# High parts of eight weight blocks taken from ScalarE to GpSimd, and the kernel's order planned anew

## The chip, the core and the metric

The kernel runs on one core of one Trainium2 chip. The metric is the device time of one execution in microseconds; the median of the three runs before the change is 571.56 us (571.51 to 574.22).

## What is computed

A block-sparse attention is followed by a channel mixer. The attention has 4 batches, 8 heads, 768 positions of 64 features, in blocks of 32 positions (24 blocks). Block rows 0 and 23 see all positions; each other row of blocks sees its two neighbours, itself, blocks 0 and 23, and three sampled blocks.

```python
scores = scale * np.matmul(q, k.transpose(0, 1, 3, 2))
mask = np.abs(blk_i - blk_j) <= window
mask = mask | (blk_i == 0) | (blk_j == 0) | (blk_i == n_blocks - 1) | (blk_j == n_blocks - 1)
# and the three sampled blocks of each row of blocks
attn = softmax(np.where(mask, scores, -1e9))
x = (attn @ v) as (batch, position, 512)
xk = mu_k * x + (1.0 - mu_k) * x_prev        # x_prev: the position before
xr = mu_r * x + (1.0 - mu_r) * x_prev
k = np.maximum(xk @ w_k, 0.0)                # w_k 512 x 1024
v = k * k @ w_v                              # w_v 1024 x 512
r = 1.0 / (1.0 + np.exp(-(xr @ w_r)))        # w_r 512 x 512
return r * v
```

The mixer's weights arrive as 64-bit floats; the kernel makes 32-bit numbers of them itself.

## The kernel before

**Attention.** There are 26 units of work (L267). Units 0 to 3 are the "wide" ones, one for each batch: block rows 0 and 23 against all positions. Units 4 to 25 are the "near" ones: one row of blocks for all four batches. A unit loads its queries (L462, DMA) and GpSimd scales them (L464); it needs keys (KA) and values (VA), which lie in two fixed tensors. The wide units fill half of KA and VA each, the near units use the same room as a ring of block slots, so a load has to wait until the matmuls that read the old contents are done. A wide unit does scores (L607), row maxima on VectorE (L616), exponentials on ScalarE (L622), transposes on TensorE (L526) with a copy out by ScalarE or VectorE (L530, L532), and the product with the values (L637). A near unit does the same in L562, L570, L542, L526, L530 and L586. finish (L646) divides by the sum (L655 to L659) and transposes into the mixer's input tiles xt (L666 to L688).

**Weights.** w_r, w_k and w_v are 20 blocks of 128 x 512: blocks 0 to 3 are w_r, 4 to 11 w_k, 12 to 19 w_v. Each block (weight, L359) is loaded as 64-bit words (L365): blocks 0 to 11 into a buffer of their own (early_w), the last eight into slots of the pool "p", which the exponentials use as well (raw). ScalarE makes a magnitude of the upper word (L374), VectorE makes the 32-bit number in three passes: a shift (L379), the sign (L383) and the tail (L387), into wf. Then the number is split in two parts for the matmuls: the high part is a rounding copy, on GpSimd (L397) for the blocks that HI_POOL (L888) names, which are 0 to 11, and on ScalarE (L399) for blocks 12 to 19; the low part is wf less the high part, on GpSimd (L401).

**Mixer.** There are 12 tiles of 256 positions. For each, split_x (L714) makes xr and xk with a difference on GpSimd (L738), a multiply-add on VectorE (L741), a rounding copy on ScalarE (L748) and a remainder on GpSimd (L750). gate does the matmuls of r (L774), hidden those of k (L792) with ReLU and square on ScalarE (L805, L806) and square and remainder on GpSimd (L807, L809), values those with w_v (L821), whose result VectorE multiplies by the gate (L829) before it is stored (L832). TensorE's work of tile t begins with the matmuls r{t}_0; they are called r0_0, r1_0 and so on here.

**Order.** Nothing is issued where it stands in the code. Each operation is added to a Plan (L86) with an engine, an assumed duration in ns, a due time (rank), the buffers that it reads and writes, and, for a load, a size. Plan.order (L190) plays the operations through with these durations and picks, for each engine, the one with the earliest due time among those that can start about then; the result is the fixed program order of each engine. The due times come from a table of numbers at the end of the file (L899 to L909): the start of each unit and tile, offsets for each kind of step, and the due times of the weights' loads (RAW_AT) and passes (WEIGHT_AT). Each engine runs its list in order and waits on semaphores, so an operation that has to wait holds up all that is behind it on its engine. SyncE (SP) issues all loads in one such list.

## Time and profile before

| | |
|---|---|
| median of the three runs | 571.56 us |
| the profiled execution's own time | 573.36 us |
| its span, first to last instruction | 571.5 us |
| busy in the span: TensorE | 538.0 us (94%) |
| busy: VectorE, ScalarE, GpSimd | 262.3, 295.2, 317.1 us |
| read from HBM | 78.60 MB |

The profiled execution took 573.36 us, 1.8 us more than the median run; its span leaves out 1.86 us around the instructions. Where a view has columns for the engines, PE is TensorE, PEld its weight loads, DVE VectorE, ACT ScalarE, POOL GpSimd, and SPq the queue of SyncE that issues DMAs. In the timeline a row has its start, its length (both us), the engine, the line, the operation, output <- input, and in brackets the idle time just before it with what ended that. In the groups by line the last columns are total busy us, mean ns of one, and the idle time before. L numbers are lines of the kernel before; in the changed kernel the same statements stand 17 lines further down (L401 is L418 there).

### The profile page before, as it was taken

To read this page: it belongs to the slowest core of one execution; us is meant where nothing else is said; L and a number is where in the kernel's file an instruction comes from. 1 tells how busy PE (TensorE), PEld (TensorE's weight loads), DVE (VectorE), ACT (ScalarE), POOL (GpSimd) and SP (SyncE) were. 2 spreads that over 40 slices of the span, in tenths; PEclk is the share of its full clock that TensorE was granted. 3 is DMA by queue.
4 is the path that set the end of the run, shared out by engine and by line. 5 is a ranking of instruction groups with operands and counts; after the bars stand their busy time and mean duration, and the time that the engine had idled before them with its cause. 6 is when DMAs were issued, how large, how long until landed. Compare 5 with 4: busy or idle time off the path is not lost.

```text
span 571.5 us, 18262 instructions
## 1 busy us (share of the span) xinstructions
PE 538.0 (94%) x7724; PEld 441.8 (77%) x7724; DVE 262.3 (46%) x481; ACT 295.2 (52%) x594; POOL 317.1 (55%) x377
## 2 busy tenths in 40 slices
PE   8678768999999999999999999999999999999997
PEld 3445545777797897897897887897798898989896
DVE  1677998864434324337325345415434424242401
ACT  2536477675656445467456456556555543424241
POOL 1322657897465384475275456466167265677670
PEclk8979998999999999999999999999999999999999
DMA  8999899734442624454543272445323000000001
GB/s 319 367 387 367 303 315 346 267 120 147 133 148 78 220 77 129 154 169 132 194 142 114 93 225 89 146 160 188 117 89 95 21 21 19 18 21 18 33 5 38
DMA packets 34181, 86.08 MB, mean 151 GB/s; under 512 B 5010, under 2 KB 5780, under 8 KB 31124
## 3 DMA queue, kind: packets, MB, share of 16 engines
q1 hardware_dynamic: 34100, 84.92, 44.2%
q8 instruction: 61, 1.00, 0.7%
q14 instruction: 20, 0.16, 0.1%
HBM read 78.60 MB, written 6.29 MB: 149 GB/s over the span
## 4 chain that ended last, share of the span: by engine, by line
PE 75%; DMA 9%; POOL 7%; DVE 4%; SPq 3%; issue 2%; ACT 1%; POOLq 0%; ACTq 0%
PE v L821 23%; PE o L586 7%; PE s L562 6%; PE t L526 6%; PE r_0p L774 5%; PE h_0p L792 5%; PE r_1p L774 5%; PE h_3p L792 5%; PE h_2p L792 5%; PE h_1p L792 5%; DMA q<-qt 3%; DMA VA<-vw 2%; DMA KA<-kt 2%; POOL q L464 2%; PE tx L666 2%
## 5 line engine op out<-in xcount | busy, mean ns | idle before, releaser
L821 PE MATMUL v<-wv,k 128*128 128x512 f32 (+1 forms) x600 | 144.8, 391 | 1.1 <-POOL wv L401 1.1
L821 PEld LDWEIGHTS v<-wv,k 128*128 128x128 f32 x600 | 106.6, 188 | 24.5 <-POOL wv L401 1.5
L542 ACT ACTIVATE p<-s,nm 128x256 f32<-128x256 f32 x176 | 71.7, 484 | 20.6 <-DVE nm L570 20.5
L464 POOL TENSOR_SCALAR q<-q 128x512 f32<-128x512 f32 (+1 forms) x26 | 36.6, 1409 | 45.8 <-DMA q<-qt 25.1
L570 DVE TENSOR_REDUCE nm<-s 128x4 f32<-128x1024 f32 x44 | 52.8, 1217 | 13.5 <-PE s L562 13.1
L530 ACT COPY pt<-t 128x512 f32<-128x512 f32 x68 | 39.6, 587 | 37.4 <-PE t L526 34.8
L526 PE MATMUL t<-ident,p 128*128 128x128 f32 x352 | 54.5, 278 | 3.8 <-ACT pt L530 2.1
L586 PEld LDWEIGHTS o<-VA,pt 128*32 128x32 f32 x2816 | 42.2, 109 | 13.3 <-issue 10.4
L586 PE MATMUL o<-VA,pt 128*32 128x65 f32 x2816 | 49.5, 222 | 2.9 <-ACT pt L530 1.9
L526 PEld LDWEIGHTS t<-ident,p 128*128 128x128 f32 x352 | 40.6, 141 | 14.8 <-ACT pt L530 2.9
L562 PE MATMUL s<-KA,q 64*32 64x256 f32 x1408 | 44.9, 383 | 4.0 <-DMA KA<-kt 1.7
L750 POOL TENSOR_TENSOR xr<-xr_1f,xr 128x256 fp32r<-128x256 f32 x24 | 17.9, 744 | 38.5 <-ACT xr L748 38.5
L829 DVE SCALAR_TENSOR_TENSOR z<-v,z 128x512 f32<-128x512 f32 (+1 forms) x25 | 16.7, 669 | 48.4 <-PE v L821 48.4
L741 DVE SCALAR_TENSOR_TENSOR xr_1f<-xr_1d,mk,xt 128x128 f32<-128x128 f32 x48 | 17.1, 355 | 47.5 <-POOL xr L750 39.7
L738 POOL TENSOR_TENSOR xr_1d<-xt 128x128 f32<-128x128 f32 x48 | 20.5, 427 | 31.8 <-DVE xr_1f L741 24.0
L792 PE MATMUL h_1p<-xk,wk 128*128 128x256 f32 x288 | 36.9, 282 | 0.0
L562 PEld LDWEIGHTS s<-KA,q 64*32 64x32 f32 x1408 | 25.2, 106 | 15.1 <-issue 2.4
L792 PE MATMUL h_0p<-xk,wk 128*128 128x256 f32 x288 | 36.8, 282 | 0.0
L774 PE MATMUL r_0p<-wr,xr 128*128 128x512 f32 x144 | 36.7, 400 | 0.0
L792 PE MATMUL h_3p<-xk,wk 128*128 128x256 f32 x288 | 36.5, 281 | 0.0
L792 PE MATMUL h_2p<-xk,wk 128*128 128x256 f32 x288 | 36.1, 281 | 0.0
L738 POOL TENSOR_TENSOR xr_0d<-xt 128x128 f32<-128x128 f32 x48 | 19.4, 403 | 30.1 <-DVE xr_0f L741 20.7
(138 smaller groups left out, 962.4 us busy)
## 6 DMA issues: line engine op xcount, KB each, us to landing
VA<-vt SPq DMA_DIRECT2D x93, 260.0 KB, 3.8
KA<-kt SPq DMA_DIRECT2D x90, 256.0 KB, 3.7
VA<-vw SPq DMA_DIRECT2D x24, 260.0 KB, 6.5
KA<-kq SPq DMA_DIRECT2D x16, 384.0 KB, 6.4
out<-z SPq DMA_DIRECT2D x23, 256.0 KB, 2.0
q<-qt SPq DMA_DIRECT2D x22, 256.0 KB, 4.3
early_w<-w_k SPq DMA_DIRECT2D x8, 512.0 KB, 7.3
raw<-w_v SPq DMA_DIRECT2D x8, 512.0 KB, 6.1
```

Of the source, the lines that this page charges most:

```text
L464: plan.add(POOL, 90 + 0.95 * HP * many * BLK, due, lambda: nc.gpsimd.tensor_scalar(out=q.ap[:, 0 : HP * many * BLK], in0=q.ap[:, 0 : HP * ...
L526: nc.tensor.transpose(tp.ap[:, i, :], p.ap[:, x : x + P], ident.ap)
L530: plan.add(ACT, 200 + 0.75 * P * many, rank + 0.1, lambda: nc.scalar.copy(pt.ap[:, 0:many], tp.ap[:, 0:many]), reads=[(tp,)], writes=[(pt,)])
L542: plan.add(ACT, 262 + 0.83 * width, rank, lambda: nc.scalar.activation(p.ap[:, out], view(), AF.Exp, bias=nm()), reads=[(s,), key[0]], wri ...
L562: nc.tensor.matmul(s.ap[ROWS[j], row, a * 256 : (a + 1) * 256].rearrange("p (c x t) -> p c t x", c=2, t=QB), q.ap[half, (hp * QB + j) * BL ...
L570: nc.vector.tensor_reduce(out=nm.ap.rearrange("p (r a) -> p r a", r=2), in_=s.ap.rearrange("p r (a x) -> p r a x", a=2), axis=AX.X, op=ALU ...
L586: nc.tensor.matmul(o[gi].ap[ROWS[j], i * DV : (i + 1) * DV], pts[row].ap[:, 2 * a + g, ROWS[j]], VA.ap[:, c0 + g, j, h * DV : (h + 1) * DV ...
L738: sub.tensor_tensor(out=parts(d.ap), in0=cols(c, 0), in1=cols(c, 1), op=ALU.subtract)
L750: plan.add(POOL, 80 + 2.4 * MIX * tw, rank + O_MIX, lambda f=f, cs=cs: nc.gpsimd.tensor_tensor(out=dst.ap[:, 1, cs], in0=f.ap, in1=dst.ap[ ...
L774: nc.tensor.matmul(pr.ap[:, 0:512], xr.ap[:, a, c, :], wr.ap[:, w, c, :], start=(c == 0 and m == 0), stop=(c == CC - 1 and m == 2))
L792: nc.tensor.matmul(ph.ap[:, ff * TT : (ff + 1) * TT], wk.ap[:, w, c, f * P : (f + 1) * P], xk.ap[:, a, c, :], start=(c == 0 and m == 0), s ...
L821: nc.tensor.matmul(pv.ap[:, 0:width], k2.ap[:, a, f, i * P : (i + 1) * P], wv.ap[:, w, f, cs], start=(f == 0 and m == 0), stop=(f == FC - ...
```

## The change

It has three parts. First, HI_POOL names blocks 0 to 19: the rounding copy of the eight blocks of w_v goes from ScalarE to GpSimd. Second, the planner's durations are changed: VectorE's passes over the weights, its multiply-adds and the packing of the sampled indices get a factor "slow", by which they are lengthened for the time in which an operation of over 300 ns stands on GpSimd beside them; some base durations and sizes of loads are changed, and the scaling of the queries is taken as 2.45 ns a column, where it was 0.95. Third, all numbers of the due-time table are new. No operation is added or removed, and apart from the eight copies none changes its engine; what each engine runs, and in which order, comes from the new plan.

```diff
+    def beside(self, at, ns, slow):
+
+        end = at + ns
+        for _ in range(4):
+            end = at + ns + slow * sum(max(0.0, min(end, b) - max(at, a)) for a, b in self.pool[-6:])
+        return end
...
+            if op.engine == "DVE":
+                vector = op
+                if op.slow:
+                    op.end = self.beside(at, ns, op.slow)
+            if op.engine == "POOL" and op.ns > 300:
+                self.pool.append((at, op.end))
+                if vector is not None and vector.slow and vector.end > at:
+                    vector.end += vector.slow * (min(vector.end, op.end) - at)
+                    free["DVE"] = vector.end
...
-                     writes=[(raw,)], release=at, size=524288)
+                     writes=[(raw,)], release=at, size=455000)
...
-            plan.add(DVE, 480, rank, shift, reads=[(mag,)], writes=[(mag,)])
-            plan.add(DVE, 800, rank, sign, reads=[(mag,), (raw,)], writes=[(mag,)])
-            plan.add(DVE, 800, rank, tail, reads=[(mag,), (raw,)], writes=[(f,)])
+            plan.add(DVE, 430, rank, shift, reads=[(mag,)], writes=[(mag,)], slow=0.53)
+            plan.add(DVE, 690, rank, sign, reads=[(mag,), (raw,)], writes=[(mag,)], slow=0.35)
+            plan.add(DVE, 690, rank, tail, reads=[(mag,), (raw,)], writes=[(f,)], slow=0.35)
...
-            plan.add(POOL, 700, rank, lambda: nc.gpsimd.tensor_copy(dst()[:, 0, :], f.ap), reads=[(f,)], writes=[(owner, (0, key))])
+            plan.add(POOL, 650, rank, lambda: nc.gpsimd.tensor_copy(dst()[:, 0, :], f.ap), reads=[(f,)], writes=[(owner, (0, key))])
...
-        plan.add(POOL, 90 + 0.95 * HP * many * BLK, due, lambda: nc.gpsimd.tensor_scalar(
+        plan.add(POOL, 90 + 2.45 * HP * many * BLK, due, lambda: nc.gpsimd.tensor_scalar(
...
-                plan.add(DVE, 2.8 * tw, rank + O_MIX, mix, reads=[(d,), (x, *ready), (mk, which)], writes=[(f, i)])
+                plan.add(DVE, 220 + 1.02 * tw, rank + O_MIX, mix, reads=[(d,), (x, *ready), (mk, which)], writes=[(f, i)], slow=0.55)
...
-HI_POOL = frozenset(range(12))
+HI_POOL = frozenset(range(20))
...
-LEAD_W, LEAD_Q, LEAD_K, LEAD_V = 9.086, 41.427, 90.995, -12.936
+LEAD_W, LEAD_Q, LEAD_K, LEAD_V = 33.654, 70.566, 88.255, -1.014
...
```

What the new plan does at three places, as the programs have it. In each piece a row is one instruction or a run of equal ones (x2), with its line, its operation, the output tile <- its inputs, and the shape.

SyncE's list before, where the keys of units 4 and 5 are loaded (KA<-kt are keys, VA<-vw values of a wide unit, raw14 is block 14, which is of w_v, q5 the queries of unit 5; the rows of L491 fetch a sampled block; the last row is the last part of unit 5's keys):

```order
L491 REGISTER_ALU x2
L491 ISA
L491 DMA KA_67<-kt 128x512
L365 DMA raw14_918<-w_v 128x1024
L462 DMA q5_945<-qt 128x512
L444 DMA KA_67<-kt 128x512
```

The same place now:

```order
L508 DMA KA_67<-kt 128x512
L479 DMA q5_848<-qt 128x512
L491 DMA VA_68<-vw 128x520 x2
L382 DMA raw16_912<-w_v 128x1024
L382 DMA raw14_919<-w_v 128x1024
L491 DMA VA_68<-vw 128x520 x4
L382 DMA raw19_962<-w_v 128x1024
L461 DMA KA_67<-kt 128x512
```

The six loads of unit 2's values, which stood ahead of unit 4's keys, now stand behind them, and three blocks of w_v instead of one stand ahead of the end of unit 5's keys.

GpSimd's list before, from the scaling of unit 8's queries on (xr0 and xk0 belong to the mixer's tile 0, xr1 to tile 1):

```order
L464 TENSOR_SCALAR q8_1481<-q8_1481 128x512
L401 TENSOR_TENSOR wv_1305<-wf12_1572,wv_1305 128x512
L738 TENSOR_TENSOR xr0_1d0_1679<-xt0_99 128x128
L750 TENSOR_TENSOR xk0_1544<-xk0f1_1585,xk0_1544 128x512
L738 TENSOR_TENSOR xr0_1d1_1736<-xt0_99 128x128
L738 TENSOR_TENSOR xr0_1d2_1758<-xt0_99 128x128
L750 TENSOR_TENSOR xr0_1_1761<-xr0_1f0_1700,xr0_1_1761 128x256
L401 TENSOR_TENSOR wv_1305<-wf18_1743,wv_1305 128x512
```

The same place now, from a few rows ahead of it:

```order
L414 CAST wv_1104<-wf15_1517 128x512
L767 TENSOR_TENSOR xk0_1554<-xk0f0_1488,xk0_1554 128x512
L418 TENSOR_TENSOR wv_1104<-wf15_1517,wv_1104 128x512
L755 TENSOR_TENSOR xk0d3_1630<-xt0_100 128x256
L481 TENSOR_SCALAR q8_1503<-q8_1503 128x512
L755 TENSOR_TENSOR xr0_1d0_1662<-xt0_100 128x128
L767 TENSOR_TENSOR xk0_1554<-xk0f1_1605,xk0_1554 128x512
L755 TENSOR_TENSOR xr0_1d1_1756<-xt0_100 128x128
L755 TENSOR_TENSOR xr0_1d2_1767<-xt0_100 128x128
L767 TENSOR_TENSOR xr0_1_1769<-xr0_1f0_1718,xr0_1_1769 128x256
L414 CAST wv_1104<-wf12_1765 128x512
L418 TENSOR_TENSOR wv_1104<-wf12_1765,wv_1104 128x512
```

Before, blocks 14 and 13 of w_v are done ahead of the row of q8, and blocks 12, 18, 16, 15, 17 and 19 follow it; now blocks 16, 14, 19, 13 and 15 are ahead of it, each with its copy, and blocks 12, 17 and 18 follow.

ScalarE's list before, around the copy of unit 7's first transposed piece (pt7_0_0), which lies behind three copies of w_v:

```order
L399 CAST wv_1305<-wf18_1743 128x512
L542 ACTIVATE p7_0_1767<-s7_0_1546,nm7_0_1608 128x256 x4
L805 ACTIVATE h0_0k_1807<-h0_0p_1745 128x512
L399 CAST wv_1305<-wf16_1790 128x512
L748 CAST xr0_1_1761<-xr0_1f1_1785 128x256
L806 ACTIVATE k20_1825<-h0_0k_1807 128x512
L530 COPY pt7_0_0_1841<-t7_0_0_1816 128x512
L399 CAST wv_1305<-wf15_1839 128x512
L530 COPY pt7_0_1_1874<-t7_0_1_1849 128x512
```

The same place now:

```order
L391 ACTIVATE wmag18_1830<-raw18_1716 128x512
L822 ACTIVATE h0_0k_1835<-h0_0p_1771 128x512
L823 ACTIVATE k20_1850<-h0_0k_1835 128x512
L765 CAST xr0_1_1769<-xr0_1f1_1805 128x256
L822 ACTIVATE h0_1k_1872<-h0_1p_1815 128x512
L559 ACTIVATE p7_1_1876<-s7_1_1607,nm7_1_1855 128x256 x4
L547 COPY pt7_0_0_1901<-t7_0_0_1879 128x512
L823 ACTIVATE k20_1850<-h0_1k_1872 128x512
L547 COPY pt7_0_1_1983<-t7_0_1_1949 128x512
```

The copies of w_v are gone from ScalarE; the exponentials of unit 7's second half (p7_1) have come ahead of pt7_0_0.

TensorE's list has the same matmuls ahead of r1_0 in both programs, in another order, and so the same ones behind it: ahead of it are all of the four wide units, 12 half units of scores (L562), 9 half units of values (L586), two gates (L774), the whole hidden part (L792) and the values part (L821) of tile 0. Ahead of r0_0 stand the same matmuls too, but for one group of four transposes (tx5, L666), which has gone behind it.

More of the change, by code (lines that the diff above doesn't have):

```diff
@@ L82 @@
 class Op:
-    __slots__ = ("engine", "ns", "lag", "fn", "rank", "deps", "users", "bufs", "end", "start", "table", "seq", "waits", "release", "size", "code", "dmas")
+    __slots__ = ("engine", "ns", "lag", "fn", "rank", "deps", "users", "bufs", "end", "start", "table", "seq", "waits", "release", "size", "code", "dmas", "slow")
 class Plan:
@@ L98, in __init__, with add @@
         self.queues = {}
-    def add(self, engine, ns, rank, fn, reads=(), writes=(), lag=0, table=None, release=0.0, size=0, code=0, dmas=1):
+    def add(self, engine, ns, rank, fn, reads=(), writes=(), lag=0, table=None, release=0.0, size=0, code=0, dmas=1, slow=0.0):
         op = Op()
@@ L105, in add @@
         op.deps, op.users, op.end, op.seq = set(), [], None, len(self.ops)
[L106 removed]
+        op.bufs, op.release, op.size, op.code, op.dmas, op.slow = [], release * 1000, size, code, dmas, slow
         for used, *keys in list(reads) + list(writes):
@@ L188, in run @@
         return self.work(end, ns * left / op.code)
+    def beside(self, at, ns, slow):
[3 more added lines that the diff above has]
+        return end
     def order(self):
+        self.pool, vector = [], None
         free, table, avail = {}, {}, {}
@@ L337, in pack @@
             v.tensor_tensor(out=packed.ap, in0=packed.ap, in1=whole[:, 0], op=ALU.bitwise_or)
-        plan.add(DVE, 5500, PICK, pack, reads=[(number,), (con,)], writes=[(r,), (e,), (packed,)])
+        plan.add(DVE, 5500, PICK, pack, slow=0.3, reads=[(number,), (con,)], writes=[(r,), (e,), (packed,)])
         for w, m in enumerate((mu_k, mu_r)):
@@ L474, in load_unit @@
                 plan.add(SP, ISSUE, at - LEAD_V, lambda g=g, c=c, part=part: nc.sync.dma_start(VA.ap[:, c, part], vw[b, g]),
-                         writes=[(VA, *[(c, part, j) for j in range(QB)])], release=at - LEAD_V, size=262144)
+                         writes=[(VA, *[(c, part, j) for j in range(QB)])], release=at - LEAD_V, size=232000)
             return q, None
@@ L897 @@
 LAST = 10
[L899 to L909 removed]
+O_MAX, O_EXP, O_TR = [729.96, 1068.75, -2659.26, 720.02], [22.35, 294.96, -481.10, 448.11], [1.48, 12.00, -243.38, -329.90]
+O_PV, O_END = [-1189.67, -125.48, -1258.70, -1272.22], [32.92, 33.70, 13.31, 331.96]
+SECOND = [7.03, 5.67, -4.63, -100.88]
+LEAD_W, LEAD_Q, LEAD_K, LEAD_V = 33.654, 70.566, 88.255, -1.014
+O_MIX, O_SQ, O_SQ_FIRST = -281.947, 1284.146, 357.911
+NEAR, STAY, STORE = 53.833, 180.777, 639.005
+UNIT_AT = [9.41, -675.38, 18.42, -388.80, 24.44, 48.97, 67.31, 88.69, 97.05, 113.73, 134.30, 147.42, 156.50, 171.87, 187.87, 208.43, 220.91, 234.15, 244.48, 264.65, 275.88, 284.12, 297.62, 339.83, 349.70, 358.79]
+MIX_AT = [79.62, 120.69, 156.49, 190.62, 227.79, 259.66, 283.93, 326.47, 362.70, 747.53, 1179.69, 1656.28]
+MIX_RATE, MIX_RATE_LAST = 1.336, 7.459
+RAW_AT = [-168.17, -329.88, -731.29, 48.63, -279.08, -219.72, -171.89, 46.34, -171.78, -945.78, -1540.07, -21.87]
+WEIGHT_AT = [4.98, -256.20, -1869.62, -233.34, -353.74, -136.35, -216.79, -196.53, -243.10, -202.23, -808.80, -274.05, 82.19, 27.81, -30.53, 59.38, -106.03, 96.35, 105.21, 27.22]
 def kernel(**inputs):
```

13 lines of the change are left out of this document (1 added, 12 removed).

## Prediction

> **What bounds the kernel now.** First the page: how busy TensorE is over the 40 slices of the span, at which clock, and how busy the DMA engines are.
>
> ```profile
> span 571.5 us, 18262 instructions
> ...
> PE   8678768999999999999999999999999999999997
> ...
> PEclk8979998999999999999999999999999999999999
> DMA  8999899734442624454543272445323000000001
> ```
>
> TensorE is full from the eighth slice on, to the last. The DMA engines are full in the first seven slices and not after them. So there are two regimes, and the change can work only where TensorE has holes. Next the stretches, cut at the start of r0_0 and of r1_0 (53 us is a cut for the loads, below), and the timeline rows that give the cuts.
>
> ```profile
> core 0: us, PE busy (x) PEld busy (x) DVE busy (x) ACT busy (x) POOL busy (x), PEclk, DMA share, GB/s
> 0.00:53.00 53.00, 39.84 (x665) 22.35 (x666) 29.10 (x58) 21.77 (x35) 13.79 (x21) 0.90 0.97 361
> 53.00:101.20 48.20, 36.17 (x924) 24.32 (x924) 45.09 (x69) 32.45 (x70) 29.08 (x31) 0.96 0.90 319
> 101.20:147.70 46.50, 43.02 (x656) 35.11 (x655) 30.46 (x52) 28.27 (x56) 37.71 (x38) 1.00 0.50 167
> 147.70:571.50 423.80, 418.98 (x5485) 359.99 (x5483) 157.69 (x304) 212.76 (x434) 236.56 (x288) 1.00 0.33 103
> ```
>
> ```profile
> 101.23 1.65 PE L774 MATMUL r_0p<-wr,xr 128*128 128x512 f32 x6
> ...
> 147.50 2.81 PE L774 MATMUL r_0p<-wr,xr 128*128 128x512 f32 x11
> ```
>
> Three stretches follow from this.
>
> The first ends at r0_0, at 101.2 us. TensorE has 25.2 us of holes (101.2 less 39.84 and 36.17), the DMA engines are 97% and 90% busy, and from 53 us on VectorE is busy for 45.09 of 48.20 us. Keys, values and weights must come in before the mixer can run.
>
> The second goes from r0_0 to r1_0 and takes 46.5 us. TensorE has 3.5 us of holes, and GpSimd is the next fullest engine with 37.71 us.
>
> The third, to the end, has 4.8 us without TensorE, of which 3.3 us lie behind its last matmul (the last gate product and store, untouched).
>
> The waits of TensorE in the second stretch and in the third name the holes:
>
> ```profile
> PE t L526 <- ACT pt L530: 1.8, 1, 1.8
> PE v L821 <- POOL wv L401: 1.1, 1, 1.1
> PE t L526 <- ACT h_3k L805: 0.4, 1, 0.4
> PE t L526 <- ACT h_0k L805: 0.2, 1, 0.2
> ...
> PE t L526 <- ACT z L781: 1.0, 1, 1.0
> PE o L586 <- DVE xk5f L741: 0.4, 1, 0.4
> ```
>
> Both orders have the same matmuls ahead of r1_0, and so the same ones behind it. Hence the end moves by as much as r1_0 moves, plus what the waits of the third stretch gain or lose. The sum is made that way.
>
> **The eight copies.** The prices of one block's steps, from the groups by line (total us, mean ns of one):
>
> ```profile
> L379 DVE TENSOR_SCALAR wmag<-wmag 128x512 int32<-128x512 int32 x20 | 14.7, 750 | 3.3 <-ACT wmag L374 3.3
> L401 POOL TENSOR_TENSOR wv<-wf,wv 128x512 fp32r<-128x512 f32 x8 | 11.0, 1376 | 1.3 <-ACT wv L399 1.3
> L383 DVE SCALAR_TENSOR_TENSOR wmag<-raw,wmag 128x512 int32<-128x512 int32 x8 | 9.3, 1160 | 0.1
> L387 DVE SCALAR_TENSOR_TENSOR wf<-raw,wmag 128x512 int32<-128x512 int32 x8 | 6.5, 806 | 1.6 <-POOL wv L401 1.5
> L397 POOL CAST wk<-wf 128x512 fp32r<-128x512 f32 x8 | 5.5, 691 | 11.3 <-DVE wf L387 9.7 <-DVE R L655 1.6
> L399 ACT CAST wv<-wf 128x512 fp32r<-128x512 f32 x8 | 4.9, 618 | 3.5 <-DVE wf L387 3.5
> ```
>
> ScalarE loses 8 x 0.618 = 4.9 us, GpSimd gains 8 x 0.691 = 5.5 us. Neither is a term by itself, since neither engine is the bound over the span; what counts is where they stood. In ScalarE's list three of these copies stood next to the copy of unit 7's first transposed piece:
>
> ```profile
> 112.40 0.62 ACT L399 CAST wv<-wf 128x512 fp32r<-128x512 f32 x1 [1.43 <-DVE wf L387]
> 113.38 0.41 ACT L748 CAST xr<-xr_1f 128x256 fp32r<-128x256 f32 x1 [0.36 <-DVE xr_1f L741]
> 113.69 0.63 ACT L806 ACTIVATE k<-h_0k 128x512 fp32r<-128x512 f32 x1
> 114.22 0.57 ACT L530 COPY pt<-t 128x512 f32<-128x512 f32 x1
> ```
>
> ScalarE stood still for 1.43 us until VectorE had finished a block, then did the copy for 0.62 us, and the piece that TensorE needed came after that. That is TensorE's 1.8 us wait. With the copy on GpSimd this holdup of 2.05 us has gone from ScalarE, and more than covers the wait: -1.8 us. The 0.2 us behind h_0k goes too, since those transposes now stand behind another hidden group. What is queued behind the same wait on GpSimd is worked out below.
>
> **Blocks done earlier.** Ahead of unit 8's queries GpSimd now has five blocks of w_v instead of two; three follow instead of six. In the second stretch GpSimd then does 3 x (0.691 + 1.376) = 6.2 us for weights where it did 6 x 1.376 = 8.3: 2.1 us less. VectorE does three blocks fewer there, each 0.750 + 1.160 + 0.806 = 2.72 us, so 8.2 us less. The matmuls with w_v waited 1.1 us for the last blocks:
>
> ```profile
> 131.70 1.31 POOL L401 TENSOR_TENSOR wv<-wf,wv 128x512 fp32r<-128x512 f32 x1 [1.28 <-ACT wv L399]
> ```
>
> GpSimd itself had stood still for 1.28 us before the last but one. With one block left behind k's remainders instead of two (block 18), and 2.1 us less ahead, that wait goes: -1.1 us. I keep the 0.4 us behind h_3k. Sum of the second stretch: -1.8 - 0.2 - 1.1 = -3.1 us. Its bounds: -3.5, all holes, and 0, if new waits fill them.
>
> **The first stretch.** VectorE's 8.2 us and GpSimd's three blocks (6.2 us) move into it. GpSimd is busy there for 13.79 + 29.08 of 101.2 us, which covers its part. VectorE has 3.1 us free after 53 us and 23.9 ahead of it. The new order uses those: eleven early blocks stand ahead of unit 4's first maximum in place of nine, so that I take its price as 0, but if the cover fails it is 8.2 - 3.1 = 5.1 us.
>
> The loads decide more. What each issues, and when SyncE got to the last part of the keys of units 5, 6 and 7:
>
> ```profile
> 70.65 0.33 SPq L444 DMA_DIRECT2D KA<-kt  x1
> 77.23 0.38 SPq L444 DMA_DIRECT2D KA<-kt  x1
> 89.46 0.52 SPq L444 DMA_DIRECT2D KA<-kt  x1
> ```
>
> ```profile
> VA<-vt SPq DMA_DIRECT2D x93, 260.0 KB, 3.8
> raw<-w_v SPq DMA_DIRECT2D x8, 512.0 KB, 6.1
> ```
>
> ```profile
> SPq L474 <- PE o L637: 3.2, 2, 3.0
> SPq L444 <- PE s L562: 2.9, 1, 2.9
> ```
>
> By the new order, 3 blocks of w_v and 4 blocks of values more lie ahead of the end of unit 6's keys: 3 x 0.524 + 4 x 0.266 = 2.64 MB, which at the 361 GB/s of the first 53 us are 7.3 us. For unit 7 it is 3 x 0.524 = 1.57 MB, 4.4 us. Against that stand SyncE's two waits between 50 and 101 us: 3.2 us for the values' room of unit 2 and 2.9 us for unit 4's scores. The new order has keys where the first wait was, and values and blocks of w_v that need not wait where the second was, so that 6.1 us of them can go. Net for unit 6: +1.2 us; for unit 7, whose scores are the last ahead of r0_0: -1.7 us. TensorE does the scores of units 6 and 7 here:
>
> ```profile
> 83.99 1.10 PE L562 MATMUL s<-KA,q 64*32 64x256 f32 x32 [0.56 <-POOL xr_0d L738]
> ...
> 95.86 1.71 PE L562 MATMUL s<-KA,q 64*32 64x256 f32 x32
> ```
>
> Neither start was released by a load, so a gain of 1.7 us there need not reach r0_0, and a loss of 1.2 us has slack between 77.23 and 83.99 to go into. I take 0 for the first stretch, with -1.7 and, if no wait goes, the 7.3 us of unit 6 as its ends.
>
> **The third stretch.** At most 1.4 us (1.0 + 0.4) can go. New waits have no row; TensorE's share is 418.98 of 420.5 us. I take 0, from -1.4 to +1.5, as many holes again as there are.
>
> **Sum.** 0 - 3.1 + 0 = -3.1 us: 573.36 to 570.3 for the profiled execution, whose own time is 1.8 us over the median of the runs; 571.56 to 568.5 for the median. A measurement of this kernel tells about 0.5% from no change, 2.9 us, so the bounds are 568.7 and 574.4, and the forecast lies just beyond the nearer one.
>
> **The rivals.** *The keys come late (slower).* Place: SyncE's list between unit 4's and unit 7's keys. If the new order only trades its waits, because unit 4's keys now stand ahead and wait for unit 2's scores themselves, the 7.3 us for unit 6 come in full and TensorE has no other work until the mixer starts. With -3.1 us after r0_0 that is +4.2: 575.8 us. It decides from the point where less than 1.5 us of the 6.1 us of waits go (7.3 - 1.5 - 3.1 = 2.7). For it: the DMA engines' 97%. Against it: 90% and 319 GB/s after 53 us, room that a list without waits would use.
>
> *GpSimd in VectorE's way (no change).* The same pass took, alone and beside GpSimd:
>
> ```profile
> 119.81 1.51 DVE L379 TENSOR_SCALAR wmag<-wmag 128x512 int32<-128x512 int32 x1
> ...
> 127.54 0.55 DVE L379 TENSOR_SCALAR wmag<-wmag 128x512 int32<-128x512 int32 x1 [0.86 <-ACT wmag L374]
> ```
>
> The eight copies could each hold a VectorE pass for their 0.691 us, 5.5 us in all; five of them fall in the first stretch, with 3.5 us where VectorE has 3.1 free after 53, and three, 2.1 us, in the second. And a copy that waits for VectorE on GpSimd holds up the scaling of queries and k's remainders, where on ScalarE it held up a transposed piece (1.43 us). Taking 2.1 of the 3.1 us back gives 570.5 us.
>
> The Trainium skill, page "SBUF — State Buffer", section "Who interferes with whom", says that VectorE in its two-port mode, or with two SBUF inputs beside a GpSimd operation that reads SBUF, shares an exclusive lock with GpSimd, and that the second to issue stands until the first is done. The trace agrees as far as the pair of rows above goes (0.55 and 1.51 us for one pass). By that rule alone, without the blocks moved earlier, the change would cost VectorE up to those 5.5 us.
>
> *The loads flow (faster still).* All 6.1 us of SyncE's waits go and TensorE's order passes on 4 of the 25.2 us of holes: 568.5 - 4 = 564.5 us. For it, a wait of TensorE in that stretch, for the values of wide units:
>
> ```profile
> PE o L637 <- DMA VA<-vw: 5.0, 8, 2.5
> ```
>
> Against it: neither of the two rows of L562 above was released by a load.
>
> *It does nothing.* The third stretch is 74% of the span and has 1.4 us of holes; if new ones of some 3 us open, 571.5 us.
>
> **How the numbers follow.** The forecast has 0.40, split about evenly by the bound that it lies next to; loads flow 0.24; GpSimd in the way and nothing together 0.15; keys late 0.21. Faster by over 0.5%: 0.24 and 0.21 of the forecast, 0.45. Within: 0.19 of it, and 0.15: 0.34. Slower: 0.21. The range goes from 563.5, a little below the case of flowing loads (-1.4 us in the third stretch would be 563.1), to 575.0, which leaves out about half of the slower case: 0.1 above and under 0.1 below.
>
> **What would show it.** Right: r1_0 starts at about 144.6 us with r0_0 still near 101, and the rows of waits on pt (1.8) and on wv (1.1) are gone between them; the stretch's TensorE holes shrink from 3.5 to about 0.4 us. SyncE's waits between 50 and 101 us fall below 3 us. Wrong: r0_0 later than 104 us with TensorE waiting for KA; or new TensorE waits on POOL in the second stretch; or more than 3 us of holes after r1_0.

## The result and the profile after

| | before | after |
|---|---|---|
| median | 572.89 us (571.51 to 574.47) | 581.32 us (579.86 to 581.87) |
| the profiled execution's own time | 573.36 us | 580.86 us |
| its span | 571.5 us | 579.0 us |
| start of r0_0 | 101.23 us | 110.15 us |
| start of r1_0 | 147.50 us | 154.26 us |

The median before is now of four runs, one more than in the table ahead of the prediction (571.56 us there). The changed kernel is slower: the ratio is 1.0142, with a 95% interval of 1.0102 to 1.0183. The prediction was 568.5 us, 563.5 to 575.0. First the page of after, the lines that answer to those of before.

```profile
PE   5767858899999999999999999999999999999997
...
PEclk9879868999999999999999999999999999999999
DMA  8999579945325444655244545611530300000001
```

TensorE is full from the ninth slice on. Ahead of that it has more holes, the clock is lower (8 and 6 in the fifth and sixth slice, where before had 9s), and the DMA engines, which were full in the first seven slices before, fall to 5 and 7 in the fifth and sixth. Next the stretches, cut at after's own r0_0 and r1_0, and the rows of these two.

```profile
core 0: us, PE busy (x) PEld busy (x) DVE busy (x) ACT busy (x) POOL busy (x), PEclk, DMA share, GB/s
0.00:53.00 53.00, 36.72 (x573) 19.54 (x573) 31.02 (x60) 20.89 (x34) 16.64 (x23) 0.90 0.97 354
53.00:110.15 57.15, 42.67 (x1016) 30.11 (x1013) 43.55 (x73) 31.84 (x69) 35.79 (x37) 0.85 0.80 287
110.15:154.26 44.11, 42.95 (x659) 36.05 (x658) 26.75 (x46) 27.44 (x57) 36.04 (x39) 1.00 0.55 187
154.26:579.00 424.74, 420.89 (x5487) 361.15 (x5485) 155.24 (x304) 211.44 (x426) 236.19 (x287) 1.00 0.32 101
```

```profile
110.15 1.64 PE L791 MATMUL r_0p<-wr,xr 128*128 128x512 f32 x6
...
154.26 1.65 PE L791 MATMUL r_0p<-wr,xr 128*128 128x512 f32 x6
```

The first stretch is 110.15 - 101.23 = 8.9 us longer. The second is 44.11 us, where before had 147.50 - 101.23 = 46.27: 2.2 us shorter. The third is 424.74 us, where before had 571.5 - 147.5 = 424.0: 0.7 us longer. So the loss lies ahead of r0_0, and a part of it is given back in the second stretch.

Of the 8.9 us, 3.4 are TensorE's own time for nearly the same matmuls (36.72 + 42.67 = 79.39 us busy, before 39.84 + 36.17 = 76.01) at a clock of 0.85 from 53 us on, where it was 0.96, and 5.5 us are holes. Who waited there? First SyncE's waits up to 110.15 us, then ScalarE's (us in total, times, longest).

```profile
SPq L461 <- PE sw L624: 6.8, 1, 6.8
SPq L470 <- PE o L654: 6.6, 1, 6.6
```

```profile
ACT wmag L391 <- DMA early_w<-w_r: 13.4, 2, 8.8
...
ACT wmag L391 <- DMA raw<-w_v: 9.3, 3, 5.1
...
ACT wmag L391 <- DMA early_w<-w_k: 7.0, 1, 7.0
```

SyncE stands for unit 2's scores (it has unit 4's keys to load) and for unit 2's products (unit 4's values), 13.4 us, where before it stood 3.2 us for room for unit 2's values and 2.9 us for unit 4's scores. ScalarE's first pass over a block (wmag) waits for weights: 29.7 us in all; while it stands there, the copies behind it in its list stand too. Before had 7.9 us of it:

```profile
ACT wmag L374 <- DMA early_w<-w_r: 7.3, 3, 3.8
...
ACT wmag L374 <- DMA early_w<-w_k: 0.6, 1, 0.6
```

How the two hang together is read from the chain that ended last, from 57 us on (start, length, what).

```profile
57.44 0.64 ACT wmag L391
...
58.92 3.44 PE sw L624 x16
...
67.00 5.28 DMA VA<-vw
...
72.35 7.89 DMA raw<-w_v
...
80.32 0.06 ACT wmag L391
...
81.35 0.48 ACT ptw L547
...
82.99 2.80 PE o L654 x96
...
85.81 0.51 SPq L470
...
87.63 5.45 DMA VA<-vt
```

It goes from a weight pass on ScalarE to unit 2's last scores (3.44 us at a low clock, 1.52 at the full one), to the values, to the load of a block of w_v (block 19, 7.89 us), to ScalarE's pass over it, to the copy of a piece of unit 2 (ptw2_0_0), which stands behind that pass and ahead of unit 2's last transposes, to unit 2's products, and only then SyncE goes on with unit 4's values. While SyncE stands, the DMA engines run dry (a share of 0.51, then 0.14): the rows below are after from 55 to 65 us, then before.

```profile
55.00:60.00 5.00, 2.10 (x28) 1.09 (x32) 2.86 (x6) 3.15 (x5) 0.26 (x1) 0.99 0.51 209
60.00:65.00 5.00, 4.67 (x68) 2.54 (x60) 3.51 (x6) 2.59 (x6) 4.15 (x4) 0.67 0.14 49
```

```profile
55.00:60.00 5.00, 4.49 (x125) 2.99 (x120) 5.00 (x7) 3.52 (x6) 2.68 (x3) 1.00 0.76 255
60.00:65.00 5.00, 3.55 (x107) 2.07 (x100) 5.00 (x7) 2.60 (x4) 3.19 (x3) 1.00 0.93 322
```

When do these loads start? Here is SyncE's list in before, then in after (start, length; the rows of KA are unit 4's keys, in the last two rows the end of unit 6's and of unit 7's keys; VA<-vw are unit 2's values).

```profile
57.18 3.75 SPq L474 DMA_DIRECT2D VA<-vw  x6
61.03 0.92 SPq L444 DMA_DIRECT2D KA<-kt  x2
```

```profile
62.39 0.93 SPq L461 DMA_DIRECT2D KA<-kt  x2
...
67.00 0.87 SPq L491 DMA_DIRECT2D VA<-vw  x2
...
92.19 0.38 SPq L461 DMA_DIRECT2D KA<-kt  x1
...
101.59 1.08 SPq L461 DMA_DIRECT2D KA<-kt  x1
```

Unit 4's keys are only 1.4 us later than in before, and TensorE's first scores of unit 4 only 0.6 us (68.46 us, before 67.84). What comes late is what stands behind the keys: unit 2's values 9.8 us, the last 96 of unit 2's products 12.4 us (82.92 us, before 70.48), and then, behind SyncE's second wait, the end of unit 6's keys 15.0 us (before 77.23) and of unit 7's 12.1 us (before 89.46). No run moves these six loads of values alone, so what their place costs by itself is not shown.

In the second stretch TensorE's waits for pt (1.8 us) and for wv (1.1 us) are gone; left are:

```profile
PE o L603 <- DMA VA<-vt: 0.6, 1, 0.6
PE h_3p L809 <- ACT h_2k L822: 0.5, 1, 0.5
```

### The profile page after: what moved, and what is told of

Its sections match the earlier page's. It is cut to its first block, busy times and chain, and to the rows that moved or that the text cites. A ratio compares the mean times of both kernels' runs of the same rounds, so it can differ in the third digit from the quotient of the medians.

```text
span 579.0 us, 18275 instructions
## 1 busy us (share of the span) xinstructions
PE 543.2 (94%) x7724; PEld 446.9 (77%) x7724; DVE 256.6 (44%) x481; ACT 291.6 (50%) x586; POOL 324.7 (56%) x385
## 4 chain that ended last, share of the span: by engine, by line
PE 77%; DMA 9%; POOL 5%; ACT 3%; SPq 2%; DVE 2%; issue 1%; POOLq 0%; ACTq 0%
PE v L838 21%; PE o L603 7%; PE t L543 6%; PE h_3p L809 6%; PE r_0p L791 5%; PE s L579 5%; PE h_2p L809 5%; PE h_1p L809 5%; PE h_0p L809 5%; PE r_1p L791 5%; DMA VA<-vt 3%; PE sw L624 2%; PE tw L543 2%; DMA q<-qt 2%; PE tx L683 1%; DMA raw<-w_v 1%
## 5 line engine op out<-in xcount | busy, mean ns | idle before, releaser
L559 ACT ACTIVATE p<-s,nm 128x256 f32<-128x256 f32 x176 | 69.8, 484 | 19.0 <-DVE nm L587 16.6
L809 PE MATMUL h_2p<-xk,wk 128*128 128x256 f32 x288 | 37.5, 283 | 0.0
L758 DVE SCALAR_TENSOR_TENSOR xr_0f<-xr_0d,mk,xt 128x128 f32<-128x128 f32 x48 | 21.9, 457 | 33.7 <-POOL xk L767 14.6
L809 PEld LDWEIGHTS h_0p<-xk,wk 128*128 128x128 f32 x288 | 35.9, 188 | 1.1
L791 PE MATMUL r_1p<-wr,xr 128*128 128x512 f32 x144 | 36.2, 397 | 0.0
```

The costliest lines, as they stand in the source:

```text
L559: plan.add(ACT, 262 + 0.83 * width, rank, lambda: nc.scalar.activation(p.ap[:, out], view(), AF.Exp, bias=nm()), reads=[(s,), key[0]], wri ...
L758: nc.vector.scalar_tensor_tensor(out=parts(f.ap[:, i, :]), in0=parts(d.ap), scalar=mk.ap[:, which, c : c + 1], in1=cols(c, 1), op0=ALU.mul ...
L791: nc.tensor.matmul(pr.ap[:, 0:512], xr.ap[:, a, c, :], wr.ap[:, w, c, :], start=(c == 0 and m == 0), stop=(c == CC - 1 and m == 2))
L809: nc.tensor.matmul(ph.ap[:, ff * TT : (ff + 1) * TT], wk.ap[:, w, c, f * P : (f + 1) * P], xk.ap[:, a, c, :], start=(c == 0 and m == 0), s ...
```

## The experiments

The theories: one, the order of the work ahead of r0_0 makes the loss; two, the copies on GpSimd make it; three, it is the price of the blocks of w_v done earlier; four, passes and loads at the head of ScalarE's and SyncE's lists; five, the loads bound the stretch in any order; six, the lowered clock.

A new plan moves everything at once, so in most kernels the engines' lists were taken from the plans and only named rows moved. The operations are the same and have the same numbers in both programs; such a kernel issues them in a written order:

```diff
-    for op in plan.order():
-        op.fn()
+    plan.order()
...
+    for i in ORDER:
+        op = plan.ops[i]
...
+        op.fn()
```

All figures in one place; r0_0 and the stretch from r0_0 to r1_0 are from one profiled execution each, the ratio is to the kernel before on the same chip.

| | r0_0, us | to r1_0, us | median, us | ratio, 95% interval |
|---|---|---|---|---|
| 1 copies alone | 102.88 | 48.50 | 577.01 | 1.0072 (1.0046 to 1.0098) |
| 2 copies back | 113.67 | 44.03 | 581.32 | 1.0120 (1.0059 to 1.0180) |
| 3 old start, new rest | 102.44 | 55.54 | 580.61 | 1.0121 (1.0068 to 1.0173) |
| 4 new start, old rest | 112.92 | 46.43 | 586.00 | 1.0207 (1.0152 to 1.0262) |
| 5 passes 3, 6 behind | 109.82 | 43.19 | 581.68 | 1.0160 (1.0133 to 1.0187) |
| 6 and 11, 1 | 113.26 | 45.14 | 582.43 | 1.0165 (1.0141 to 1.0189) |
| 7 three blocks later | 106.24 | 58.44 | 592.12 | 1.0341 (1.0310 to 1.0373) |
| 8 holes filled | 109.31 | 43.23 | 579.47 | 1.0129 (1.0095 to 1.0162) |
| 9 the fifth mended | 113.27 | 43.38 | 580.38 | 1.0132 (1.0097 to 1.0167) |
| 10 nine and seven | 107.45 | 60.12 | 593.91 | 1.0375 (1.0339 to 1.0412) |
| 11 before, piece ahead | 101.56 | 46.69 | 572.80 | 0.9994 (0.9975 to 1.0013) |
| 12 and holes filled | 101.75 | 46.70 | 573.85 | 1.0019 (0.9997 to 1.0040) |
| 13 old up to 48 us | 114.62 | 45.69 | 583.83 | 1.0181 (1.0154 to 1.0207) |
| 14 new up to 45 us | 114.77 | 49.52 | 592.61 | 1.0338 (1.0309 to 1.0368) |
| 15 values first | 111.20 | 46.03 | 580.46 | 1.0125 (1.0098 to 1.0151) |
| 16 before, less on GpSimd | 100.36 | 46.06 | 572.75 | 0.9994 (0.9978 to 1.0011) |
| 17 three repairs | 108.53 | 57.81 | 593.07 | 1.0344 (1.0307 to 1.0381) |
| 18 eleven and sixteen | 101.08 | 46.68 | 573.66 | 1.0000 (0.9980 to 1.0021) |

The fourth has the same lists as after ahead of r0_0, but for the four transposes tx5, which stand ahead of it again, and starts it at 112.92 instead of 110.15 us; the last transposes that both have there start 1.3 us apart (111.06 and 109.74 us). The four executions of the second lie between 578.49 and 584.71 us. So a difference of under some 3 us in one execution's r0_0 says little here, and I go by groups below.

### The copies (1, 2)

```diff
-            plan.add(ACT, 520, rank, lambda: nc.scalar.copy(dst()[:, 0, :], f.ap)
+            plan.add(ACT, 520, rank, lambda: nc.gpsimd.tensor_copy(dst()[:, 0, :], f.ap)
```

The plan still takes them for ScalarE's, so that nothing else moves. 

> The kernel before with its order untouched; only the eight copies of w_v are issued on GpSimd, at the same places. Theory one (the order of the work ahead of r0_0 makes the loss, the copies do not): r0_0 at 101 to 102 us, TensorE's 1.8 us wait for pt between r0_0 and r1_0 gone, 570 to 573 us beside 572.9 before. Theory two (the copies stand in VectorE's and GpSimd's way): five copies ahead of r0_0 and three behind it cost up to 5.5 us of VectorE's time, r0_0 at 104 us or later, 575 to 578 us.

Measured: 0.72% slower than before. The copies alone, in the old order, cost 4 us (by the interval 2.6 to 5.6): half the loss of the whole change, and theory two has a part in it. From r0_0 to r1_0 it took 48.50 us (before 46.27); TensorE's wait for pt did not go. The rows: that wait, and what ScalarE did ahead of the copy of the piece.

```profile
PE t L526 <- ACT pt L530: 2.0, 1, 2.0
```

```profile
115.45 0.41 ACT L748 CAST xr<-xr_1f 128x256 fp32r<-128x256 f32 x1 [3.15 <-DVE xr_1f L741]
```

The copy of w_v no longer holds ScalarE, but the next row of its list does, for 3.15 us, until VectorE has the difference from GpSimd. GpSimd has hardly a gap there, as its windows show (POOL is the fifth engine): in the first experiment, and, for the same piece of its list, in before.

```profile
101.93:133.32 31.39, 29.41 (x470) 24.53 (x463) 23.28 (x35) 18.31 (x39) 29.67 (x30) 0.92 0.54 176
```

```profile
100.97:130.42 29.45, 27.07 (x463) 22.75 (x463) 22.71 (x35) 19.72 (x42) 27.05 (x26) 1.00 0.59 198
```

It works 29.67 of 31.39 us: four more rows, 2.6 us more work, and the piece takes 1.9 us longer.

```diff
-            plan.add(POOL, 650, rank, lambda: nc.gpsimd.tensor_copy(dst()[:, 0, :], f.ap)
+            plan.add(POOL, 650, rank, lambda: (nc.gpsimd.tensor_copy if i < 12 else nc.scalar.copy)(dst()[:, 0, :], f.ap)
```

> The kernel after with its order untouched; only the eight copies of w_v are issued on ScalarE again, at the same places. Theory one (the order ahead of r0_0): r0_0 at 110 us as in the kernel after (110.15), 580 to 582 us beside 572.9 before. Theory two (the copies): the 1.3 us wait of TensorE for GpSimd ahead of unit 7's scores goes and VectorE's passes get shorter, r0_0 at 105 us or earlier, 575 to 578 us.

Measured: 581.32 us, as long as after. In the new order no difference is seen by who copies; the intervals (1.0059 to 1.0180, and 1.0102 to 1.0183 for after) leave room for some 4 us, so that the order absorbs the copies' price is likely and not shown. What is shown is that the new order is slower than before without these copies on GpSimd too.

### Halves exchanged (3, 4)

The cut is by emission: all that one plan issues ahead of r0_0, then what is left in the order of the other. 

> Everything that the kernel before issues ahead of r0_0 (by its plan) in the order of before, all the rest in the order of after, and the copies on GpSimd. Theory one: r0_0 at 101 to 102 us, then 44.1 to 46.5 us to r1_0, 570 to 573 us. Theory two: as in the first experiment, 575 us or more. Theory three (the gain of 2.2 us behind r0_0 is bought by blocks of w_v done earlier, ahead of it): r0_0 at 101 us, but 46.5 us or more to r1_0, since GpSimd has five or six blocks left in place of three; 573 to 575 us.

> The reverse: everything that the kernel after issues ahead of r0_0 in its order, all the rest in the order of before, and the copies on GpSimd. Theory one: r0_0 at 110 us, 580 to 584 us. Theory two: it is the copies and not the order, 575 to 578 us. Theory three: r0_0 at 110 us, and 44 us or less to r1_0, 580 to 582 us.

Measured: the old start gives r0_0 at 102.44 us, the new one at 112.92. What is ahead of r0_0 is decided by these lists, as theory one has it. But the old start with the new rest needs 55.54 us to r1_0, with one long wait:

```profile
PE o L603 <- DVE pt L549: 8.3, 1, 8.3
```

The new rest counts on blocks 15, 16 and 19 being done; they now stand behind r0_0, and VectorE does them ahead of a piece that TensorE needs (for 4.42 of the 8.3 us it stands itself, for ScalarE's pass over one of them). This is theory three, in a clear form: the shorter second stretch is paid for ahead of r0_0. The blocks alone do not shorten it either: in the fourth they are done ahead of r0_0 and the rest has the old order, and the stretch takes 46.43 us, as before (46.27).

### What holds up the start (5, 6, 9, 7, 10, 15, 13, 14, 17)

In the fifth, ScalarE's passes of blocks 3 and 6 go behind four of its rows (here with block numbers in place of the tiles' numbers), and VectorE's six passes behind unit 2's last maximum.

```diff
-L391 wmag3, wmag6
 L639 pw2_1_0, pw2_1_1
 L547 ptw0_1_2, ptw0_0_0
+L391 wmag3, wmag6
 L391 wmag9, wmag7, wmag5
 L547 ptw0_0_2
```

> The kernel after; of blocks 3 and 6 ScalarE's pass now stands behind the copies of unit 0's transposed pieces that it stood ahead of, and VectorE's six passes behind unit 2's last maximum. Theory four (a pass that waits for its weights holds up ScalarE, so unit 2's scores, so SyncE's keys of unit 4, and the loads stand idle from 55 to 65 us): unit 2's last scores start at 55 to 56 us instead of 58.9 and run at the full clock, unit 4's scores 4 to 5 us earlier than 68.5, r0_0 at 105 to 107 us instead of 110.15, 576 to 578 us. Theory five (the loads bound the stretch whatever the order): r0_0 at 109 us or later, 580 to 581 us.

Measured: unit 2's last scores at 55.96 us in 1.52 us, as theory four has it. But a new hole of 4.39 us followed at 59 us, and r0_0 came at 109.82. ScalarE's pass of block 7 had no buffer until VectorE was done with block 3. The sixth adds the same for blocks 11 and 1, behind the three copies to xt, ptw3_1_0 and pw3_0. 

> As the run before, and ScalarE's passes of blocks 11 and 1 too stand behind the copies and exponentials of unit 1 and 3 that they stood ahead of (TensorE waited 5.3 us there, at 32 us). Theory four: up to 5 us more, if nothing else is late there; but at 45 us the kernel after is only 3.1 us of TensorE's work behind the kernel before, so at most about 3 us more: r0_0 at 102 to 105 us, 573 to 576 us. Theory five: no gain from it, since unit 3's values land at about 44 us in any case: r0_0 as in the run before.

Measured: the wait at 32 us (5.3 us) went, and TensorE waited 8.5 us for unit 3's and unit 2's values (5.2 in after) and 5.3 us for keys (none in after) instead; r0_0 at 113.26. Neither theory's number. The ninth mends the fifth:

```diff
-L391 wmag3, wmag6
 L639 pw2_1_0, pw2_1_1
 L547 ptw0_1_2, ptw0_0_0
-L391 wmag9, wmag7, wmag5
+L391 wmag3, wmag6
 L547 ptw0_0_2
+L391 wmag9
 L639 pw2_0_0, pw2_0_1
 L547 ptw2_1_0
+L391 wmag7
 L547 ptw2_1_2
+L391 wmag5
```

> The fifth experiment mended. There the earlier scores of unit 2 were gained (55.96 us, full clock), but ScalarE then stood for 3.5 us ahead of block 7 until VectorE was done with block 3, and TensorE 4.4 us for a piece of unit 0. Now ScalarE's passes of blocks 3, 6, 9, 7 and 5 each stand behind the pieces of units 0 and 2 that TensorE needs first, and VectorE's passes of 3 and 6 behind the copy of unit 0's piece. Theory four (head of ScalarE's list, then SyncE's keys): unit 4's scores at 64 to 65 us instead of 68.5, unit 2's values in time, r0_0 at 105 to 107 us, 575 to 578 us. Theory five (the loads): r0_0 at 109 us or later, 580 us or more.

Measured: unit 4's first scores at 63.62 us, 4.8 us earlier than in after, and all of it lost again 5 us later, at VectorE:

```profile
69.91 1.12 PE L543 MATMUL tw<-ident,pw 128*128 128x128 f32 x4 [4.61 <-DVE ptw L549]
```

```profile
65.00:70.00 5.00, 0.39 (x4) 0.15 (x3) 5.00 (x8) 0.93 (x2) 2.67 (x3) 0.73 1.03 392
```

VectorE (third) is busy for 5.00 of 5.00 us with passes over weights, and the copy of a piece waits its turn. Theory four is right about each wait and wrong about the sum. In the seventh, all rows of blocks 15, 16 and 19 (the loads L382, the passes L391, L396, L400, L404, L414, L418) stand behind r0_0 on each engine. 

> The kernel after, with the loads and all passes of blocks 15, 16 and 19 moved behind the start of r0_0, in the same order among themselves. Theory three (the loss ahead of r0_0 is the price of three blocks moved there: 1.57 MB of loads and 8.2 us of VectorE): r0_0 at 104 to 106 us, and 4 us or more added behind it. Theory four: r0_0 at 108 us or later, since the stall at 53 to 62 us lies ahead of these blocks.

The tenth is the ninth and the seventh together. 

> The run before, and blocks 15, 16 and 19 with their loads behind r0_0 as in the seventh experiment (which put r0_0 at 106.24 us). If the two causes are separate and add up, 3.9 us for the blocks and 4 to 5 us for the waits: r0_0 at 101 to 103 us, as in the kernel before (101.23). If both are the same loads seen twice: r0_0 at 105 to 106 us. The end says nothing here, since the three blocks then hold up what follows (592 us in the seventh).

Measured: r0_0 at 106.24 and 107.45 us. The ninth's repair added nothing to the seventh. In the fifteenth, the six loads of unit 3's values stand ahead of unit 0's (L491, the run of twelve), with the sixth's move of blocks 11 and 1 only. 

> The kernel after with ScalarE's passes of blocks 11 and 1 behind the pieces of units 1 and 3 as in the sixth experiment (but not those of blocks 3 and 6), and with the six loads of unit 3's values ahead of the six of unit 0's on SyncE, as the kernel before has them. In the sixth experiment TensorE then waited 8.5 us for values. If this order of the loads is what makes TensorE 3.1 us late at 45 us: unit 3's transposes at 46 to 48 us instead of 50.7, r0_0 at 106 to 108 us. If not: r0_0 at 109 us or later.

Measured: unit 3's transposes at 47.51 us, 3.2 us earlier than in after and level with before; then 3.53 us lost ahead of unit 2's last scores (58.23 us, after 58.92), and r0_0 at 111.20. Thirteen and fourteen cut the lists earlier, by emission as in the third and fourth. 

> All that the kernel before issues ahead of the transposes of unit 3's result (47.6 us there, 50.7 us in the kernel after) in the order of before, all the rest in the order of after. If the loss arises ahead of that point and carries on: unit 3's transposes at 47 to 48 us and r0_0 at 105 to 107 us. If it arises behind it, at the stall of SyncE for unit 2's scores and at the three blocks: r0_0 at 109 to 111 us.

> The reverse: all that the kernel after issues ahead of unit 0's last scores (45.2 us in both kernels) in its order, the rest in the order of before, copies on GpSimd. Beside it stands the first experiment (102.88 us with the old order alone). If the loss arises early: r0_0 at 105.5 to 107 us. If it arises behind 45 us: r0_0 at 102.5 to 104 us.

Measured: 114.62 and 114.77 us, worse than either kernel. In the thirteenth the old start was ahead by 5 us at 46 us, and all of that went ahead of unit 2's last scores (56.56 us). ScalarE's row, TensorE's, and the 14.5 us ahead of VectorE's maximum:

```profile
55.56 1.76 ACT L639 ACTIVATE pw<-sw,nmw 128x768 f32<-128x768 f32 x2 [9.78 <-DVE nmw L633]
...
56.56 3.64 PE L624 MATMUL sw<-KA,q 64*64 64x384 f32 x16 [10.22 <-ACT pw L639]
```

```profile
40.00:54.50 14.50, 5.78 (x126) 3.23 (x122) 13.79 (x17) 4.01 (x6) 10.14 (x10) 0.82 1.01 366
```

TensorE waits for ScalarE, ScalarE for VectorE's maximum, and VectorE (third) is busy for 13.79 of the 14.50 us ahead of that: the passes of blocks 1, 4, 11 and 8, which the old start had not done yet, stand ahead of the maximum in the new rest. In the fifteenth the same scores waited for something else, ScalarE's pass over block 3, which waited for its load:

```profile
56.16 1.22 ACT L391 ACTIVATE wmag<-early_w 128x512 f32<-128x512 f32 x2 [7.12 <-DMA early_w<-w_r]
```

In the fourteenth TensorE stands for 7.52 us ahead of 55.73 us, for a piece on VectorE. Neither half of a list is good with the other; the loss has no single place before or behind 45 us. The seventeenth has the repairs of nine, fifteen and seven at once. 

> The kernel after with the repairs of runs 9, 15 and 7 at once: ScalarE's passes of blocks 11 and 1, and of 3, 6, 9, 7 and 5, behind the pieces that TensorE needs first, with VectorE's passes of 3 and 6 behind them; unit 3's values loaded ahead of unit 0's; blocks 15, 16 and 19 with their loads behind r0_0. If the loss is a chain of these limits: unit 3's transposes at 47.5 us, unit 4's scores at 61 to 63 us, r0_0 at 102 to 104 us. If something else sets r0_0 too (VectorE's passes of the other blocks, the room of keys and values): r0_0 at 105 to 107 us as in runs 7 and 10. The end says nothing, as in those.

Measured: unit 3 at 47.47, unit 4's scores at 62.51, then 4.62 and 3.81 us for VectorE and 2.96 us for keys, r0_0 at 108.53. So it is a chain, but with more links than three. By groups: the eight kernels with the new lists and all blocks ahead of r0_0 (after, 2, 4, 5, 6, 8, 9, 15) have it at 109.3 to 113.7 us, mean 111.7; the three without blocks 15, 16 and 19 (7, 10, 17) at 106.2 to 108.5, mean 107.4; the seven with the old lists (before, 1, 3, 11, 12, 16, 18) at 100.4 to 102.9, mean 101.6. Three blocks moved ahead cost some 4.3 us; the other 5.8 us belong to the order, and which row of it carries them stays open. Theory five is not ruled out for the three blocks: their 1.57 MB are, by the prediction's own working, 4.4 us of loading. For the order it does not hold, since the old lists start r0_0 at 101.6 us, and in after the DMA engines stand nearly idle from 60 to 65 us.

### The clock (8, 12)

```diff
+        unit_of, many = FILL.get(op.seq, (0, 0))
+        for i in range(many):
+            nc.tensor.matmul(spare[unit_of].ap[:, 260:512], one[:, 0:P], one[:, 0:252], start=True, stop=True, skip_group_check=True)
         op.fn()
```

> The kernel after with 70 matmuls of 128x252 bf16 that nobody reads, put where TensorE stood still: 18 ahead of unit 2's last scores, 28 and 8 ahead of its products, 16 ahead of unit 4's. Theory six (3.4 us of the loss are a lower granted clock behind the holes: TensorE's busy time up to r0_0 is 79.4 us instead of 76.0 for the same matmuls): unit 2's last scores take 1.5 us instead of 3.4, the clock from 60 to 100 us is above 0.9, r0_0 at 107 to 108 us, 578 to 579 us. If the waits set the pace and not the clock: 580 to 582 us.

Measured: the clock from 53 us to r0_0 is 0.97 instead of 0.85, r0_0 comes at 109.31, the span is 577.0 instead of 579.0 us, and the ratio, 1.0129 (1.0095 to 1.0162), can't be told from after's 1.0142. The clock is about 2 of the 7.5 us or less: where the clock is full, TensorE waits longer instead. The twelfth is read with the eleventh. 

> The run before, with 48 matmuls of 128x252 bf16 that nobody reads ahead of three holes of TensorE (16 at 8 us, 18 at 31 us, 14 at 92 us), so that the clock isn't lowered behind them (0.66 from 10 to 15 us, 0.50 from 35 to 40, 0.66 from 95 to 100 in the kernel before). In the eighth experiment such matmuls took 2.0 us off the span of the kernel after. If the clock sets the pace there: 1 to 2 us less than the run before. If the loads do: the same as the run before.

Measured: the same as the eleventh. But the clock did not rise: up to r0_0 it is 0.93, in the eleventh 0.95. So this run does not say what the clock is worth in the old order.

### The second stretch (11, 16, 18)

All three are the kernel before with small moves. Eleven, ScalarE's list (names as above):

```diff
 L805 h0_0k
+L530 pt7_0_0
 L399 wv (block 16)
 L748 xr0_1
 L806 k20
-L530 pt7_0_0
```

> The kernel before, its copies on ScalarE as they were; in ScalarE's list the copy of unit 7's first transposed piece stands right behind the copy of the first hidden group, ahead of a copy of w_v, of a copy of xr and of a square, which it stood behind. The second step of the prediction took 1.8 us of TensorE's wait for that piece as due to the copy of w_v; the first experiment removed this copy and the wait stayed (1.98 us), because the copy of xr behind it then stood for 3.15 us until VectorE was done. If the place in the list makes the wait: the wait goes, r1_0 at 145.7 to 146.5 us instead of 147.5, 570 to 571.5 us. If GpSimd sets the pace of that stretch (it is full from 101 to 140 us): the wait goes, TensorE waits as long for w_v instead, 572 to 573 us.

Measured: the wait for pt is gone, and the stretch takes 46.69 us. TensorE's waits there now:

```profile
PE v L821 <- POOL wv L401: 1.0, 1, 1.0
PE t L526 <- ACT h_3k L805: 1.0, 1, 1.0
PE o L586 <- DVE x L659: 0.8, 1, 0.8
PE t L526 <- ACT h_0k L805: 0.5, 1, 0.5
```

3.3 us, where before had 3.5. Sixteen takes eight differences off GpSimd:

```diff
-                    sub.tensor_tensor(out=parts(d.ap)
+                    (nc.vector if name in ("xr0_1", "xr1_0") else sub).tensor_tensor(out=parts(d.ap)
```

> The kernel before; the eight differences of 128x128 of tile 0's second and tile 1's first half of xr (2.7 and 1.8 us on GpSimd between 104 and 138 us) are issued on VectorE at the same places. If GpSimd sets the pace between r0_0 and r1_0: the last block of w_v is done 3 to 4 us earlier than 136.5 us, r1_0 at 145 to 146.5 us instead of 147.5, 569.5 to 571.5 us. If VectorE is as full there as GpSimd (30.5 of 46.5 us before): no gain, 572 to 573 us.

Measured: the wait for wv is gone, 46.06 us, no gain: 1.6 us for pt, 0.9 for a piece on VectorE. 

> The kernel before with the edits of runs 11 and 16 together: the first piece of unit 7 ahead of three rows of ScalarE's list, and eight differences on VectorE. Run 11 took away the 1.8 us of TensorE's wait for the piece and got 46.7 us from r0_0 to r1_0; run 16 took away the 1.1 us for w_v and got 46.1; before has 46.3. If these two waits hide each other and nothing else does: 43.5 to 45 us from r0_0 to r1_0, 570 to 571.5 us. If a third one is behind them (VectorE's maxima and results, the ReLU of the last hidden group): 45.5 us or more, 572 to 573 us.

Measured: 46.68 us and a ratio of 1.0000 (0.9980 to 1.0021). With both away, VectorE's result of unit 6 is next:

```profile
117.22 1.47 PE L586 MATMUL o<-VA,pt 128*32 128x65 f32 x64 [2.00 <-DVE x L659]
```

Three engines are late by about the same there. No kernel was found that is faster than before.

## Why the prediction was wrong

**Ahead of r0_0.** The step that failed is the one on SyncE: "so that 6.1 us of them can go". They did not go, they became 13.4 us: the end of unit 6's keys came 15.0 us later and not 1.2, the end of unit 7's 12.1 us later and not 1.7 earlier. I had looked at what the two waits were for, and that the new list had other rows at their places. I had not asked what the new rows wait for: unit 4's keys for unit 2's scores, and unit 4's values for unit 2's products, whose values now stand behind the keys, four of the six loads behind two blocks too. Nor were the two waits all that SyncE stood for there: the same view of before has 3.5 us for VectorE (L365) and 1.9 us for a near unit's products (L453), which the working left out. The rival "the keys come late" says just that of the keys. It was right in its sign and its place, but not in its price (4.2 us, where the median rose by 8.4) nor in its last link: unit 4's keys were hardly late, and TensorE did not wait for KA, but for values, for pieces behind ScalarE's weight passes, and for VectorE.

**The blocks moved earlier** were priced at 0, with 5.1 us if VectorE's cover fails. They cost some 4.3 us, and in the chain of after it is not VectorE first: block 19's load of 7.89 us stands ahead, through ScalarE's pass, of a piece of unit 2. The prediction followed the three blocks on SyncE, VectorE and GpSimd and left out their passes on ScalarE, where 29.7 us of waiting for weights (before 7.9) now stand ahead of other copies. That is the second gap in the working. VectorE's cover is thin as well: with ScalarE's waits out of the way (nine, ten and seventeen), it holds TensorE for 4.6 us.

**The second stretch** was forecast at -3.1 us and came to -2.2, with both waits gone as said. The size was near by luck, the cause was not the one named. The first experiment removed the copies from ScalarE and the wait for pt stayed; the eleventh removed the wait and the stretch stayed. What shortened it was the new order together with three blocks done ahead of it: with the blocks still to do, the new order takes 55.54 us (third), and with them done, the old order takes 46.43 (fourth). That GpSimd gains 5.5 us and is "the next fullest engine" stood in the text; its price was taken as covered. In the old order it is 4 us for the whole kernel.

**The third stretch**, 0 with bounds of -1.4 and +1.5, came to +0.7.

**GpSimd in VectorE's way** was the wrong rival for the right engine. VectorE's passes did not become longer; in after the groups are:

```profile
L396 DVE TENSOR_SCALAR wmag<-wmag 128x512 int32<-128x512 int32 x20 | 9.9, 502 | 19.0 <-ACT wmag L391 18.7
...
L400 DVE SCALAR_TENSOR_TENSOR wmag<-raw,wmag 128x512 int32<-128x512 int32 x8 | 6.0, 758 | 0.1
```

A shift takes 502 ns on average where it took 750, a sign of w_v 758 where it took 1160: the new order keeps more of these passes apart from GpSimd (10 of the 20 shifts have GpSimd at work beside them, in before 14), and VectorE's busy time falls from 262.3 to 256.6 us. The rule of the Trainium skill, page "SBUF — State Buffer", section "Who interferes with whom", on which I laid 5.5 us, holds for instructions that meet; in the first experiment, where the copies stand in the old order, VectorE was busy for 263.1 us, 0.8 more than before. So the plan did what its new factor asks for. It bought time on an engine that was not last. The prediction's pair of rows does not show a shift alone, either: beside the one of 0.55 us, from 127.54 us on, GpSimd was still at work until 127.80 us; the shortest shift of before took 0.40 us.

**The range** ended at 575.0. The upper end of the first stretch, +7.3 us, stood in the text "if no wait goes"; it was left out of the range because I took the waits to be going.

## What to carry to other kernels

Of a queue that stands still, ask of each row that moves to the place of a wait what it waits for itself, and follow a moved step on every engine that it touches, the one that only prepares it too: an early pass whose data is late holds up all that is behind it. Where several engines are equally late, a wait that is removed shows up elsewhere with the same length, so that neither the wait nor its removal is worth what the row says. Price one part of a change in the unchanged order before a new order is planned around it: the copies alone were 4 us, and the new order cost 1.2% (0.6 to 1.8) without them.
